# Attention and two mixture layers in one kernel: fills off GpSimd, a new order of first loads, a longer held-back tail

## The chip, the cores and the metric

The kernel runs on one core of one Trainium2 chip. The metric is the device time of one execution in microseconds (us); less is better.

## The reference

Three steps follow one another on 2304 tokens of width 512:

```python
attn_out = _attn_ref(q, k, v)            # 4 x 8 heads, 576 x 64, causal, window 64
x = moe(x): h = x @ w_in; r = relu(h); return (r * r) @ w_out       # 512 -> 2048 -> 512
x = moe2(x):
    do_compute = x @ w_skip > 0
    e_idx = argmax(x @ w_gate)           # 8 experts
    y[mask] = gate_w * (relu(x[mask] @ w1[e]) @ w2[e])              # 512 -> 1024 -> 512
    out[do_compute] = x + y
```

All of it is in float32; each float32 product is made of three matmuls on a high and a low half of the operands.

## The kernel before, in words

The tokens stand in 18 tiles of 128 (t), two tiles to a chunk (c, nine chunks). Engines are named as in the profile: PE (TensorE, with PEld for its weight loads), DVE (VectorE), ACT (ScalarE), POOL (GpSimd), SP (SyncE, which issues most loads).

**Opening (0 to about 45 us).** Attention of chunks 0 and 1 runs as eight groups (a tile and half of its heads). For one group: `at_qk` puts a mask (L261) and the scores (L278) into PSUM, DVE takes the maximum (L288, and the small L291 on 128x4), ACT the four exponentials (L302), DVE the sum and its reciprocal (L306, L308) and the product (L309). `at_tr` transposes the result on PE (L317) and copies it with ACT (L319). `at_pv` multiplies by v (L335), and ACT and DVE write the high and low half of the first layer's input `xt` (L343, L344).

In the same stretch the weights of the first mixture layer are converted from the 64-bit floats in which they come, in 32 halves (`conv_next`): ACT scales (L220), POOL clamps (L221), DVE does three integer steps on 128x512 (L223, L225, L227), ACT rounds to the high half (L233), POOL subtracts (L234). Behind each L234 a small POOL memset (L205) releases the load of a later half. `HOMES` says which of three buffers holds q and k of a tile; `load_next` loads the next tile into a buffer when it comes free. Tile 6 is the first that uses the zero-padded `qpad`, whose two 64x512 zero fills (L160, L161) are on POOL. `setup_routing` makes the constants of the routing step, and a 128x512 fill (L146) that a DMA from ACT's queue (L147) spreads over the routing table in DRAM.

**Middle.** For each chunk and each of eight units j: `l1` (first layer, 24 matmuls of 256 columns on L464 to L466, then relu L483, square L489, high half L490, low half L491) and, two units later, `l2` (12 matmuls of 512 columns, six for each tile). The results of `l1` stand in pool `gp`. Attention of later chunks and the routing are put between.

**Tail of the last chunk.** `l2` of the last `TAIL` units is held back. In a part whose order is written out by hand, tile 0 gets its six matmuls of each held-back unit first, then routing of tile 0 runs beside tile 1's matmuls. The first expert block follows.

**Experts (531 us to the end).** Each of eight experts has one block of 128 tokens (`static`), and extra blocks (`extras`) behind a branch, where more than 128 tokens go to it. A block begins with `ex_x`: four transposes (L818), a copy to the high half (L729) and a subtraction for the low half (L730), then the matmuls L831. In the profile three extra blocks run, one for expert 0 and two for expert 1.

The order of the instructions on each engine in the opening and the middle is set by a scheduler when the program is built; the engines then run their lists in that order.

Of the kernel before, what the change touches and what calls it, by code (L numbers as in the profile page):

```python
# [19 lines left out]
P = 128  # L20
# [27 lines left out]
DOT00 = 6  # L48
ROW = NE * NT
FILLS = ((2, 3), (1, 2), (1, 0), (2, 3), (2, 0), (0, 5))  # L50
TAIL = 3
FE = 1024
KF = FE // P
WIN = 64
# [8 lines left out]
def body(ctx, tc, qt_d, kt_d, vw_d, wi_d, wo_d, w9_d, w9r_d, w1_d, w2_d, out):  # L63
# [10 lines left out]
    small = pool("small", 4)  # L74
    xtp = pool("xtp", 2)
    rp = pool("rp", 2)
    gp = pool("gp", 3)
    dram = pool("dram", 1, space=DRAM)
    ps_h = pool("ps_h", 2, space=PSUM)
    ps_acc = pool("ps_acc", 1, space=PSUM)  # L80
# [15 lines left out]
    def sm():  # L96
        return sp.tile([P, 512], F32, tag="sm", name="sm")
# [35 lines left out]
            out=mask.rearrange("p a b -> p (a b)"), in_=maskb.rearrange("p a b -> p (a b)"))  # L133

    def setup_routing():
        nc.gpsimd.memset(ones, 1.0)
        nc.gpsimd.memset(tri, 1.0)
        nc.gpsimd.affine_select(
            out=tri, in_=tri, pattern=[[1, P]], compare_op=ALU.is_gt,
            fill=0.0, base=0, channel_multiplier=-1)  # L140
        nc.gpsimd.iota(io8i, pattern=[[1, NE]], base=0, channel_multiplier=0)
        nc.gpsimd.tensor_copy(out=io8, in_=io8i)
        nc.gpsimd.iota(route[:, :, 0], pattern=[[P, NT]], base=0, channel_multiplier=1)
        nc.gpsimd.memset(ohsum[:, 0, :], 0.0)
        fill = sm().bitcast(I32)
        nc.gpsimd.memset(fill, FAR)  # L146
        nc.scalar.dma_start(  # L147
            out=tab_v.rearrange("p r c -> p (r c)"), in_=fill[:, 0:2 * ROW])
        nc.scalar.dma_start(out=w9, in_=w9_d)
# [6 lines left out]
    def load_qk(t):  # L156
        i = home(t)
        k_ = kvs[i > 0].tile([P, NPAIR, P + WIN], F32, tag=f"k{i}", name="k")
        if t == len(HOMES):
            nc.gpsimd.memset(qpad[0:64, :, 1, :], 0.0)  # L160
            nc.gpsimd.memset(qpad[64:128, :, 0, :], 0.0)  # L161
        if t < len(HOMES):
            nc.sync.dma_start(
                out=q_s[i], in_=qt_d[t].rearrange("h d a b -> (h d) a b"))
        else:
            for h in range(2):
                nc.sync.dma_start(out=qpad[64 * h:64 * h + 64, :, h, :], in_=qt_d[t, h])
        nc.sync.dma_start(out=k_, in_=kt_d[t])
        kt_t[t] = k_

    def load_v(t):
        i = home(t)
        v_ = kvs[i > 0].tile([P, 2, DM], F32, tag=f"v{i}", name="v")
        nc.sync.dma_start(out=v_, in_=vw_d[t])
        vw_t[t] = v_

    def load_next(t, load):
        later = [n for n in range(t + 1, NT) if home(n) == home(t)]
        if later:
            load(later[0])  # L180
# [75 lines left out]
    def at_qk(t, g):  # L256
        s = bank("qk", t, g)
        i, k_ = home(t), kt_t[t]
        early = t // CT in EARLY
        if early:  # L260
            nc.tensor.matmul(  # L261
                s.rearrange("p (a b) -> p a b", a=2), lhsT=identb,
                rhs=mask_of(t, maskb).unsqueeze(1).to_broadcast([P, 2, 2 * P]),
                start=True, stop=False, skip_group_check=True)
        for pi in range(2):
            for blk in range(2):
                u = 2 * pi + blk
                pr = 2 * g + pi
                cols = slice(u * P, (u + 1) * P)
                if t >= len(HOMES):  # L270
                    nc.tensor.matmul(
                        s[:, cols], lhsT=qpad[:, 2 * pr + blk].rearrange("p a b -> p (a b)"),
                        rhs=k_[:, pr, 64 * blk:64 * blk + P],
                        start=not early, stop=True, skip_group_check=early)
                    continue
                for h in range(2):
                    half = slice(64 * h, 64 * h + 64)
                    nc.tensor.matmul(  # L278
                        s[half, cols], lhsT=q_s[i][half, 2 * pr + blk],
                        rhs=k_[half, pr, 64 * blk:64 * blk + P],  # L280
                        start=not early, stop=True, skip_group_check=early)
        if g == 1:
            load_next(t, load_qk)
        ef = sm()
        e = ef.rearrange("p (a b) -> p a b", a=4)
        nmx = small.tile([P, 4], F32, tag="nmx", name="nmx")
        if early:
            nc.vector.tensor_reduce(  # L288
                out=nmx, in_=s.rearrange("p (a b) -> p a b", a=4), axis=AX.X, op=ALU.max,
                negate=True)  # L290
            nc.vector.tensor_scalar(  # L291
                out=nmx, in0=nmx, scalar1=1.0 / 8.0, scalar2=None, op0=ALU.mult)
        else:
            mk = mask_of(t, mask)
            for u in range(4):
                nc.vector.tensor_tensor_reduce(  # L296
                    out=e[:, u, :], in0=s[:, u * P:(u + 1) * P],
                    in1=mk[:, u % 2 * P:(u % 2 + 1) * P], scale=-1.0 / 8.0, scalar=HUGE,
                    op0=ALU.add, op1=ALU.min, accum_out=nmx[:, u:u + 1])
        sums = small.tile([P, 4], F32, tag="sum", name="sum")  # L300
        for u in range(4):
            nc.scalar.activation(  # L302
                out=e[:, u, :], in_=s[:, u * P:(u + 1) * P] if early else e[:, u, :],
                func=AF.Exp, bias=nmx[:, u:u + 1],
                scale=1.0 / 8.0 if early else -1.0, accum_out=sums[:, u:u + 1])
        nc.vector.tensor_scalar(  # L306
            out=sums, in0=sums, scalar1=1e-9, scalar2=None, op0=ALU.add)
        nc.vector.reciprocal(out=sums, in_=sums)  # L308
        nc.vector.tensor_tensor(  # L309
            out=e, in0=e, in1=sums.unsqueeze(2).to_broadcast([P, 4, P]), op=ALU.mult)  # L310
        p_t[t, g] = e
# [287 lines left out]
    if True:  # L599
# [8 lines left out]
        load_qk(0)  # L608
        conv_load()
        load_qk(1)  # L610
        load_v(0)
        conv_load()
        load_qk(2)
        load_v(1)
        conv_load()
        load_v(2)
        conv_load()
        for _ in range(LOOK - 4):
            conv_load()
        setup_masks()  # L620
        acc_pool[1] = ps_s
        qk, tr, pv = grp_ops(0)
        qk1, tr1, pv1 = grp_ops(1)
# [3 lines left out]
        for s in range(10):  # L627
            if s < 8:
                qk[s]()
            if 1 <= s < 9:  # L630
                tr[s - 1]()
            if 2 <= s:
                pv[s - 2]()
            for _ in range(PRO[s]):
                conv_next()
            if s == 4:
                setup_routing()

        def w_free(kind, j):
            slot_q.extend((wp, w_tag[kind, j, h]) for h in range(2))  # L640
# [172 lines left out]

        def ex_x(tx, inner=True):
            xg = tx[2]
            pp = psa()
            for k in range(KD):
                nc.tensor.transpose(pp[:, k * P:(k + 1) * P], xg[:, k * P:(k + 1) * P], ident)  # L818
            return ex_split(pp, inner)

        def ex_block(e, tx, xt, fill=lambda i: None, nxt=lambda: None, late=False):
            ti, gw, xg, _ = tx
# [176 lines left out]
```

## Time and profile before

| | |
|---|---|
| time, median of 3 runs (lowest, highest) | 686.37 us (684.65, 687.01) |
| the profiled execution: its own time, its span | 685.27 us, 683.6 us |
| PE busy, share of the span | 656.6 us, 96% |
| DVE / ACT / POOL busy | 415.3 / 357.5 / 155.4 us |
| mean granted TensorE clock | 0.989 |
| DMA moved | 88.72 MB |

The span runs from the first to the last instruction. Idle time counts on the engine that the others wait for, here PE in most of the span; the mean hides that the first 45 us and the last 180 us look different from the middle.

### The profile page before, as it was taken

The page shows a single profiled execution, that of the slowest core. Times are in us where ns is not written, and L with a number is a line of the kernel's source. Part 1 is how long each engine was busy: PE and PEld are TensorE (multiplying, and loading weights), DVE is VectorE, ACT ScalarE, POOL GpSimd, SP SyncE. Part 2 cuts the span into 40 slices and gives each one's busy share as a digit, 9 for nine tenths or more (in the row PEclk, how much of TensorE's full clock was granted, in tenths as well). Part 3 has the DMA queues.
Part 4 walks back from the last instruction along what each step waited for, and adds up shares of the span by engine and source line. Part 5 has one row for each costly group of instructions (what it writes and reads, how often), then busy time and mean ns, then how long its engine had stood idle before and what let it go on. Part 6 is the DMA issues. An engine that isn't in the chain of part 4 may idle for free. (4 is left out here: it accounts for less than half of the span.)

```text
span 683.6 us, 12514 instructions
## 1 busy us (share of the span) xinstructions
PE 656.6 (96%) x4569; PEld 566.7 (83%) x4569; DVE 415.3 (61%) x1200; ACT 357.5 (52%) x821; POOL 155.4 (23%) x185
## 2 busy tenths in 40 slices
PE   7799999999999999999999999999999999999995
PEld 4588888989899889898989989899988777777774
DVE  4999977449627727716725824942735644288981
ACT  4887756544535444635535444544641544277761
POOL 5557666100100100000000000030001513044641
PEclk9899999999999999999999999999999999999998
DMA  8965453053203203203112121206592347559500
GB/s 332 349 206 172 147 168 111 1 203 98 70 32 102 70 32 101 70 32 102 40 61 85 48 71 50 83 26 230 177 317 100 111 151 279 224 161 337 222 12 8
DMA packets 45605, 88.72 MB, mean 130 GB/s; under 512 B 17806, under 2 KB 18062, under 8 KB 45392
## 3 DMA queue, kind: packets, MB, share of 16 engines
q1 hardware_dynamic: 42112, 83.38, 35.6%
q0 software_dynamic: 2976, 3.95, 1.8%
q8 instruction: 47, 0.77, 0.5%
q10 hardware_dynamic: 432, 0.32, 0.2%
q14 instruction: 38, 0.31, 0.1%
HBM read 79.07 MB, written 12.49 MB: 134 GB/s over the span
## 5 line engine op out<-in xcount | busy, mean ns | idle before, releaser
L464 PE MATMUL h<-xt,wi 128*128 128x256 f32 x576 | 165.3, 287 | 2.1 <-ACT r L480 2.1
L465 PE MATMUL h<-xt,wi 128*128 128x256 f32 x576 | 165.6, 287 | 0.3 <-DVE xt L344 0.3
L466 PE MATMUL h<-xt,wi 128*128 128x256 f32 x576 | 164.0, 285 | 0.0
L464 PE MATMUL acc<-wo,gh 128*128 128x512 f32 x288 | 116.3, 406 | 1.1 <-ACT gh L490 1.0
L464 PEld LDWEIGHTS h<-xt,wi 128*128 128x128 f32 x576 | 110.6, 192 | 6.4 <-ACT r L480 3.1
L465 PEld LDWEIGHTS h<-xt,wi 128*128 128x128 f32 x576 | 110.6, 192 | 3.4 <-DVE xt L344 0.6
L465 PE MATMUL acc<-wo,gh 128*128 128x512 f32 x288 | 112.6, 393 | 0.0
L466 PE MATMUL acc<-wo,gl 128*128 128x512 f32 x288 | 112.0, 393 | 0.0
L491 DVE TENSOR_TENSOR gl<-r,gh 128x512 fp32r<-128x512 f32 x72 | 52.4, 728 | 96.5 <-ACT gh L490 95.0
L466 PEld LDWEIGHTS h<-xt,wi 128*128 128x128 f32 x576 | 110.7, 192 | 0.0
L456 POOL DMA_INDIRECT tab_d<-route,posi x18 | 19.5, 1084 | 362.6 <-DVE posi L447 263.7
L483 ACT ACTIVATE r<-h 128x512 f32<-128x512 f32 x58 | 34.5, 595 | 98.4 <-PE h L466 94.7
L375 DVE CUSTOM_DVE_ANT_0 prod<-sm,w9b 128x512 f32<-128x512 f32 x108 | 74.0, 685 | 1.9 <-ACT sm L352 1.5
L466 PEld LDWEIGHTS acc<-wo,gl 128*128 128x128 f32 x288 | 54.1, 188 | 12.6 <-DVE gl L491 0.8
L464 PEld LDWEIGHTS acc<-wo,gh 128*128 128x128 f32 x288 | 54.1, 189 | 11.1 <-ACT gh L490 2.1
L465 PEld LDWEIGHTS acc<-wo,gh 128*128 128x128 f32 x288 | 54.3, 189 | 8.6 <-issue 0.2
L548 DVE TENSOR_TENSOR e_s<-e_s,e_s 128x1024 fp32r<-128x1024 f32 x34 | 42.1, 1258 | 11.9 <-ACT e_s L546 11.5
L302 ACT ACTIVATE sm<-sm,nmx 128x128 f32<-128x128 f32 x96 | 37.5, 392 | 20.7 <-DVE nmx L296 20.3
L319 ACT COPY sm<-a 128x512 f32<-128x512 f32 x36 | 21.4, 594 | 48.8 <-PE a L317 48.8
L489 ACT ACTIVATE r<-r 128x512 f32<-128x512 f32 x72 | 45.6, 634 | 1.5
L490 ACT CAST gh<-r 128x512 fp32r<-128x512 f32 x72 | 44.6, 619 | 1.5
L546 ACT CAST e_s<-e_s 128x1024 fp32r<-128x1024 f32 x42 | 42.9, 1050 | 2.5 <-PE acc L466 2.0
(205 smaller groups left out, 1144.6 us busy)
## 6 DMA issues: line engine op xcount, KB each, us to landing
e_s<-in_w_dram SPq DMA_DIRECT2D x54, 512.0 KB, 6.4
v<-in_vw_dram SPq DMA_DIRECT2D x18, 512.0 KB, 3.4
ri<-in_wi_dram SPq DMA_DIRECT2D x16, 512.0 KB, 4.1
ro<-in_wo_dram SPq DMA_DIRECT2D x16, 512.0 KB, 3.7
k<-in_kt_dram SPq DMA_DIRECT2D x18, 384.0 KB, 4.2
e_r<-in_w_dram SPq DMA_DIRECT2D x10, 512.0 KB, 6.6
x_d<-sm SPq DMA_DIRECT2D x17, 256.0 KB, 2.5
out_dram<-sm SPq DMA_DIRECT2D x17, 256.0 KB, 3.1
```

Of the source, the lines that this page charges most:

```text
L302: nc.scalar.activation(out=e[:, u, :], in_=s[:, u * P:(u + 1) * P] if early else e[:, u, :], func=AF.Exp, bias=nmx[:, u:u + 1], scale=1.0 ...
L319: nc.scalar.copy(out=pt, in_=pp)
L375: nc.vector.tensor_tensor_reduce(out=prod, in0=x2_t[t], in1=w9b_t[0][:, j, :], scale=1.0, scalar=0.0, op0=ALU.mult, op1=ALU.add, accum_out ...
L464: nc.tensor.matmul(out_ap, lhsT=ah, rhs=bh, start=start, stop=False)
L465: nc.tensor.matmul(out_ap, lhsT=ah, rhs=bl, start=False, stop=False)
L466: nc.tensor.matmul(out_ap, lhsT=al, rhs=bh, start=False, stop=stop)
L483: nc.scalar.activation(out=r, in_=hp.rearrange("p a b -> p (a b)"), func=AF.Relu)
L489: nc.scalar.activation(out=r, in_=r, func=AF.Square)
L490: nc.scalar.copy(out=ghf, in_=r)
L491: nc.vector.tensor_tensor(out=glf, in0=r, in1=ghf.bitcast(F32), op=ALU.subtract)
L546: nc.scalar.copy(out=hi, in_=raw)
L548: eng.tensor_tensor(out=lo, in0=raw, in1=hi.bitcast(F32), op=ALU.subtract)
```

## The change

Constants: `TAIL` goes from 3 to 4, pool `gp` from 3 to 4 buffers (the fourth holds the results of the one more unit), and the scratch of POOL's DMAs from 8192 to 4096 bytes.

```diff
     def setup_routing():
-        nc.gpsimd.memset(ones, 1.0)
-        nc.gpsimd.memset(tri, 1.0)
+        nc.vector.memset(ones, 1.0)
+        nc.vector.memset(tri, 1.0)
...
-        nc.gpsimd.memset(ohsum[:, 0, :], 0.0)
+        nc.vector.memset(ohsum[:, 0, :], 0.0)
         fill = sm().bitcast(I32)
-        nc.gpsimd.memset(fill, FAR)
+        nc.vector.memset(fill, FAR)
...
-        if g == 1:
+        if g == 1 and t != 2:
             load_next(t, load_qk)
+        if g == 1 and t == len(HOMES) - 1:
+            load_next(2, load_qk)
...
         load_qk(0)
         conv_load()
         load_qk(1)
+        conv_load()
         load_v(0)
+        load_qk(2)
         conv_load()
-        load_qk(2)
         load_v(1)
         conv_load()
         load_v(2)
-        conv_load()
         for _ in range(LOOK - 4):
             conv_load()
         setup_masks()
+        setup_routing()
...
-            if s == 4:
-                setup_routing()
...
         def ex_x(tx, inner=True):
             xg = tx[2]
+            if inner:
+                return ex_x_halves(xg)
...
+        def ex_x_halves(xg):
+            hi = gp.tile([P, 512], F32R, tag="gh", name="xh2")
+            lo = gp.tile([P, 512], F32R, tag="gl", name="xl2")
+            pps = [psa(), psa()]
+            cut = [slice(n * 256, (n + 1) * 256) for n in range(2)]
+            for n in range(2):
+                for k in range(2):
+                    nc.tensor.transpose(
+                        pps[n][:, k * P:(k + 1) * P],
+                        xg[:, (2 * n + k) * P:(2 * n + k + 1) * P], ident)
+                nc.scalar.copy(out=hi[:, cut[n]], in_=pps[n][:, 0:256])
+            for n in range(2):
+                nc.vector.tensor_tensor(
+                    out=lo[:, cut[n]], in0=pps[n][:, 0:256], in1=hi[:, cut[n]].bitcast(F32),
+                    op=ALU.subtract)
+            return hi, lo
```

`ex_x_halves` serves the extra blocks alone; a `static` block's tokens still go through `ex_x` whole. After the change the line numbers of the attention are two higher (L304 for L302, L321 for L319, L346 for L344 and so on).

The scheduler gives other lists for the opening. At three places:

**ACT, its first instructions.** `ri` is the raw half of a first-layer weight, `sm` the scores of a group. Before:

```order
L220 ACTIVATE ri_0_138<-ri_0_138 128x512
L302 ACTIVATE sm,sum<-s,nmx 128x128 x4
L220 ACTIVATE ri_1_145<-ri_1_145 128x512
L302 ACTIVATE sm,sum<-s,nmx 128x128 x4
L233 CAST wi_0_298<-f 128x512
L220 ACTIVATE ri_0_152<-ri_0_152 128x512
```

and now:

```order
L147 DMA tab_d<-sm 128x288
L220 ACTIVATE ri_0_138<-ri_0_138 128x512
L220 ACTIVATE ri_1_143<-ri_1_143 128x512
L304 ACTIVATE sm,sum<-s,nmx 128x128 x8
L233 CAST wi_0_309<-f 128x512
L220 ACTIVATE ri_0_150<-ri_0_150 128x512
L233 CAST wi_1_406<-f 128x512
L220 ACTIVATE ri_1_154<-ri_1_154 128x512
```

The scaling of the second weight half (L220 on `ri_1`) has moved ahead of the exponentials of the first two groups, the fourth ahead of the first copy L321, and the DMA of the routing table (L147) to the front.

**POOL, where `qpad` is zeroed.** Before:

```order
L221 TENSOR_SCALAR ri_1_156<-ri_1_156 128x512
L221 TENSOR_SCALAR ro_0_158<-ro_0_158 128x512
L161 MEMSET qpad 64x8x64
L160 MEMSET qpad 64x8x64
L234 TENSOR_TENSOR wi_0_507<-f,wi_0_507 128x512
L205 MEMSET ri_1_510 128x2
L146 MEMSET sm 128x512
L221 TENSOR_SCALAR ro_1_301<-ro_1_301 128x512
```

and now:

```order
L221 TENSOR_SCALAR ro_0_158<-ro_0_158 128x512
L221 TENSOR_SCALAR ro_1_312<-ro_1_312 128x512
L234 TENSOR_TENSOR wi_1_576<-f,wi_1_576 128x512
L205 MEMSET ro_0_579 128x2
L161 MEMSET qpad 64x8x64
L160 MEMSET qpad 64x8x64
L221 TENSOR_SCALAR ri_0_409<-ri_0_409 128x512
L221 TENSOR_SCALAR ri_1_504<-ri_1_504 128x512
```

The fill `sm` (L146) is gone from here. The two fills of `qpad` stand behind the subtraction of the fourth weight half, and before it stand two clamps.

**DVE, from the third to the fourth half of `xt`.** Before:

```order
L344 TENSOR_TENSOR xt<-xp,xt 128x2x128
L291 TENSOR_SCALAR nmx<-nmx 128x4
L227 SCALAR_TENSOR_TENSOR f<-ro_0_158,h_118 128x512
L308 RECIPROCAL sum<-sum 128x4
L288 TENSOR_REDUCE nmx<-s 128x4
L344 TENSOR_TENSOR xt<-xp,xt 128x2x128
```

and now:

```order
L346 TENSOR_TENSOR xt<-xp,xt 128x2x128
L310 RECIPROCAL sum<-sum 128x4
L223 TENSOR_SCALAR h_118<-ri_0_409 128x512
L290 TENSOR_REDUCE nmx<-s 128x4
L311 TENSOR_TENSOR sm<-sm,sum 128x512
L225 SCALAR_TENSOR_TENSOR h_118<-ri_0_409,h_118 128x512
L293 TENSOR_SCALAR nmx<-nmx 128x4
L227 SCALAR_TENSOR_TENSOR f<-ri_0_409,h_118 128x512
L346 TENSOR_TENSOR xt<-xp,xt 128x2x128
```

Between the same two rows there now stand a whole conversion (three wide steps on `ri_0`) and a product L311. Over the opening DVE's list has, ahead of the product of the eighth group (L309, now L311), 29 conversion steps where it had 21, eight maxima and eight products as before, and five writes of `xt` where it had six. On PE, 24 first-layer matmuls of 256 columns stand ahead of the eighth group's transposes where 36 stood.

## Rows read from the trace of the kernel before

**Rows 1.** Busy time by stretch: us, busy (instructions) of each engine, TensorE clock, DMA share, GB/s.

```profile
0.00:45.00 45.00, 35.38 (x344) 25.68 (x345) 34.25 (x74) 30.64 (x103) 23.47 (x51) 0.89 0.86 304
45.00:500.00 455.00, 453.37 (x3354) 406.99 (x3354) 277.02 (x982) 236.83 (x596) 72.92 (x96) 1.00 0.29 94
500.00:531.00 31.00, 29.87 (x225) 25.84 (x224) 12.88 (x54) 8.18 (x16) 4.85 (x5) 1.00 0.57 205
```

**Rows 2.** Timeline of TensorE: start, us, engine, line, [idle before it and its releaser].

```profile
28.89 0.38 PE L261 MATMUL s<-maskb,identb 128*128 128x512 bf16 x1 [1.47 <-ACT sm L302]
...
42.02 0.28 PE L465 MATMUL h<-xt,wi 128*128 128x256 f32 x1
42.14 0.28 PE L466 MATMUL h<-xt,wi 128*128 128x256 f32 x1
...
42.97 0.66 PE L317 MATMUL a<-ident,sm 128*128 128x128 f32 x4
```

**Rows 3.** Two stretches of 2 us, columns as in the first group.

```profile
10.00:12.00 2.00, 1.40 (x17) 0.94 (x17) 2.00 (x7) 1.06 (x5) 0.00 (x0) 1.00 1.04 413
...
32.00:34.00 2.00, 1.73 (x9) 1.46 (x10) 2.00 (x7) 1.94 (x10) 0.45 (x1) 0.50 1.11 342
```

**Rows 4.** Timeline of VectorE in the opening.

```profile
7.88 0.69 DVE L288 TENSOR_REDUCE nmx<-s 128x4 f32<-128x512 f32 x1 [6.63 <-PE s L278]
...
14.78 0.54 DVE L291 TENSOR_SCALAR nmx<-nmx 128x4 f32<-128x4 f32 x1
...
24.34 2.90 DVE L291 TENSOR_SCALAR nmx<-nmx 128x4 f32<-128x4 f32 x1
...
27.87 0.69 DVE L225 SCALAR_TENSOR_TENSOR h<-ri,h 128x512 int32<-128x512 int32 x1
28.47 0.16 DVE L306 TENSOR_SCALAR sum<-sum 128x4 f32<-128x4 f32 x1
...
35.17 0.84 DVE L291 TENSOR_SCALAR nmx<-nmx 128x4 f32<-128x4 f32 x1
...
41.91 0.69 DVE L309 TENSOR_TENSOR sm<-sm,sum 128x512 f32<-128x512 f32 x1
```

**Rows 5.** Timeline of GpSimd beside VectorE's long wait.

```profile
24.32 0.52 POOL L160 MEMSET qpad<- 64x512 f32 x1
24.81 1.27 POOL L234 TENSOR_TENSOR wi<-f,wi 128x512 fp32r<-128x512 f32 x1
...
26.06 0.52 POOL L146 MEMSET sm<- 128x512 int32 x1
26.56 0.66 POOL L221 TENSOR_SCALAR ro<-ro 128x512 f32<-128x512 f32 x1
```

**Rows 6.** Timeline of ScalarE in the opening.

```profile
8.87 0.37 ACT L302 ACTIVATE sm<-s,nmx 128x128 f32<-128x128 f32 x1 [1.01 <-DVE nmx L291]
...
11.32 0.69 ACT L220 ACTIVATE ri<-ri 128x512 f32<-128x512 f32 x1 [0.94 <-DMA ri<-in_wi_dram]
```

**Rows 7.** Timeline of TensorE at the end of the last chunk.

```profile
512.28 0.39 PE L466 MATMUL acc<-wo,gl 128*128 128x512 f32 x1
513.68 0.50 PE L464 MATMUL acc<-wo,gh 128*128 128x512 f32 x1 [1.00 <-ACT gh L490]
```

**Rows 8.** Timeline of ScalarE there.

```profile
511.40 1.05 ACT L546 CAST e_xt<-e_s 128x1024 fp32r<-128x1024 f32 x1
...
513.01 0.62 ACT L490 CAST gh<-r 128x512 fp32r<-128x512 f32 x1
```

**Rows 9.** Timeline of TensorE at the start of an extra block.

```profile
570.10 0.63 PE L818 MATMUL a<-ident,sm 128*128 128x128 f32 x4 [0.95 <-DVEq L900]
571.45 0.50 PE L831 MATMUL h<-e_xt,xh 128*128 128x512 f32 x1 [0.72 <-ACT xh L729]
```

**Rows 10.** Timeline of ScalarE: the copy of 512 columns there.

```profile
570.81 0.59 ACT L729 CAST xh<-a 128x512 fp32r<-128x512 f32 x1 [2.65 <-PE a L818]
```

**Rows 11.** Timeline of ScalarE: a copy of 256 columns in the opening.

```profile
28.72 0.38 ACT L343 CAST xt<-xp 128x256 fp32r<-128x256 f32 x1
```

More of the change, by code (lines that the diff above doesn't have):

```diff
@@ L50 @@
 FILLS = ((2, 3), (1, 2), (1, 0), (2, 3), (2, 0), (0, 5))
-TAIL = 3
+TAIL = 4
 FE = 1024
@@ L76, in body @@
     rp = pool("rp", 2)
-    gp = pool("gp", 3)
+    gp = pool("gp", 4)
     dram = pool("dram", 1, space=DRAM)
@@ L983 @@
     nc = bacc.Bacc("TRN2", target_bir_lowering=False, num_devices=1,
-                   dynamic_dma_scratch_size=8192)
+                   dynamic_dma_scratch_size=4096)
     arrays, args = {}, []
```

## The prediction

> **What bounds the kernel now.** I read the busy time by stretch first, because the mean over the span hides where there is anything to win. From 45 to 500 us TensorE is busy for 453.37 of 455.00 us at full clock, so 1.6 us are idle there; from 500 to 531 us it is 29.87 of 31.00 [rows 1]. No edit can win in the middle. In the first 45 us TensorE is busy for 35.38, idle for 9.6, and its mean granted clock is 0.89 [rows 1]. That stretch, the end of the last chunk and the starts of the expert blocks are the three places that the change touches, and I take them one by one.
>
> In the opening, look at two stretches: from 10 to 12 us the DMA queues are full (413 GB/s), and from 32 to 34 us TensorE is granted 0.50, its 1.2 GHz level [rows 3], after a stretch with holes: the largest ended at 28.89, 1.47 us long, behind the exponentials [rows 2]. Then ask who paces it. The opening ends for TensorE with the eighth group's transposes at 42.97, which stand behind VectorE's eighth product, 41.91 to 42.60 [rows 2, 4]. So I follow VectorE from its first maximum at 7.88 to 42.5: 34.6 us. A wide step takes 0.60 at its pace (27.87 to 28.47) [rows 4]; its list holds 37 wide steps there (21 conversion steps, eight maxima, eight products), 22.2 us, and about 4.2 us of `xt` writes and small steps. It works for 26.4 us and stands for 8.2.
>
> Part of that standing is one small instruction, L291 on 128x4. A step of that size takes 0.16 (L306), but L291 took 2.90, 0.84 and 0.54 at three places [rows 4], 3.8 us over the normal price. During the longest GpSimd ran without a gap, and L291 ended at 27.24, when GpSimd's last clamp of that run did (26.56 + 0.66) [rows 4, 5].
>
> **Scale.** The profiled execution took 685.27 us and the median is 686.37, 1.1 higher. The sum is made against 685.27, and 1.1 is added at its end. A measurement of this kernel can tell some 0.3% from no change, 2.06 us: below 684.3 is faster, above 688.4 slower.
>
> **End of the last chunk.** TensorE waits 1.00 us there for the high half `gh` of the last unit [rows 7]. ScalarE writes it from 513.01 to 513.63, behind a cast of 1.05 us for the next expert's weights [rows 8]. With four units held back instead of three, tile 0's matmuls of one more unit stand ahead of that wait: six of about 0.24 us (512 columns, at twice the 0.12 from 42.02 to 42.14 for 256 [rows 2]), 1.4 us of work which is not new, only moved. So the wait is covered, and about 0.1 that follows it for the low half: -1.1, with bounds from -1.1 to 0 (nothing, if the cast still stands ahead of `gh`). The fourth `gp` buffer costs no time. Two loads of expert weights move behind stores on SyncE's queue, but are used some 80 us later: 0. The early gather of tile 0 has up to 0.5 us less slack; what covers it is the matmul work of tile 1, and if that ran out the cost would be that 0.5.
>
> **Extra blocks.** From the first transpose of a block to its first matmul now pass 1.35 us: 570.10 to 571.45, of which 0.72 is idle behind the copy [rows 9]. The copy of 512 columns takes 0.59 [rows 10], one of 256 columns 0.38 [rows 11]. With halves the first copy starts when two of the four transposes are done, and the first matmul needs that half alone: about -0.18 for two transposes and -0.21 for the copy, 0.4 a block. Three extra blocks run. For expert 0's a full copy for the next block goes ahead on ScalarE, so I count 0.2 there: 0.4 + 0.4 + 0.2, -1.0, bounds -1.2 to 0. One more copy and one more subtraction a block lie beside the matmuls: 0.
>
> **Opening, what is added.** VectorE's list now has 29 conversion steps ahead of the eighth product where it had 21, and one `xt` write fewer: 8 x 0.60 - 0.3 = +4.5. TensorE has 24 first-layer matmuls ahead of the eighth transposes where it had 36; what no longer fills holes runs later, 12 x 0.12 (42.02 to 42.14) [rows 2]: +1.4. The fills now on VectorE stand ahead of 7.88, where it waited 6.63 us for scores [rows 4]: 0. On ScalarE the second weight half's scaling now stands ahead of the first exponentials, which began at 8.87; it began at 11.32, when its data landed [rows 6]. The `v` load moves behind it, 512 KB at 413 GB/s or 1.27 us earlier, and the table's fill of 144 KB moves in front, 0.36 later; so about 10.4, and the exponentials of the first groups come about 11.0. Eight exponentials of 0.37 then follow without a break, to 14.0; before, the second four came behind the scaling, from 12.01 to 13.5. So they end 0.5 later, and VectorE has conversion steps to fill that time. I count it among the stalls below. TensorE may start later by up to the 2 us, which the same holes hold.
>
> **Opening, what is taken.** Three instructions of 0.52 like L160 and L146 leave GpSimd's run beside L291 [rows 5]: the two `qpad` fills move behind the fourth subtraction, the routing fill to VectorE. By the row L291 waited for the whole run, so it gets 3 x 0.52 shorter: -1.6. The other 6.6 us in which VectorE stood (8.2 less 1.6) have nothing to do in the list of before; in the new one eight conversion steps stand among them. All of them filled would be -6.6, none 0. No row tells which, and I take half, -3.3.
>
> The opening: 4.5 + 1.4 - 1.6 - 3.3 = +1.0. Its bounds: if nothing is filled and the fills were not what L291 waited for, +5.9; if VectorE never stands, -2.3.
>
> What L291 waits for can be read in a second way. The row shows 2.90 us across the ends of four GpSimd instructions, at about 24.8, 26.1, 26.6 and 27.2 [rows 5]. The Trainium skill, "SBUF — State Buffer", section "SBUF: two separate sides", says that VectorE and GpSimd lock their shared pair of ports for one whole instruction and the other blocks; by it L291 would get in at the first end, after 0.5 us. By that rule the removed fills would be worth nothing and the sum would be 1.6 higher. The trace doesn't agree with a lock that is let go at each end, and I go by the row.
>
> The scratch of GpSimd's DMAs at half the size: the trace of before shows no stall that it could lengthen, and only a few of these DMAs are under way at once; 0, and up to 0.5 for the gathers of an expert if it turns them into a wait.
>
> **Sum.** 685.27 + 1.0 - 1.1 - 1.0 = 684.2 in the profiled execution's scale, 685.3 in that of the median.
>
> **Rivals.**
>
> *Fills were not the cause.* L291 waited for the clamps and subtractions in that run, and these are still there: 685.3 + 1.6 = 686.9, still within 0.3%. Chance 0.06, counted with the forecast below.
>
> *Faster: the opening gets shorter.* All three long L291 go, so the other 2.2 us of their price are won whole instead of half (-1.1), and with fewer holes TensorE is not granted 0.50 from 32 to 34 us [rows 3], which costs 1.0 there at half speed: 685.3 - 2.1 = 683.2, between 681.5 and 684.3 as more of VectorE's standing is filled. For it: the routing's GpSimd work goes to the start, where GpSimd is idle. Against: in the new lists more VectorE work precedes each group, and groups pace TensorE. Chance 0.36.
>
> *Slower: a new long wait of the small step.* GpSimd now runs two clamps, the subtraction of the fourth half and both `qpad` fills one behind another: 2 x 0.66 + 1.27 + 2 x 0.52 = 3.6 us [rows 5], where it ran for 2.9 beside the L291 of before. If the L291 (now L293) of the fifth or sixth group falls to its start, it waits for all of it, VectorE's longer list stands behind it, and exponentials, transposes and `xt` follow. Then nothing of 1.6 is won, and of the 6.6 only 1.1 instead of 3.3: opening +4.8, 685.3 + 3.8 = 689.1, between 688.4 and 690.5. It decides when VectorE still stands for more than 6.4 of its 8.2 us in all before the eighth product: then the opening is 5.9 - 1.8 = 4.1 longer, and the sum 688.4. For it: the fills are still on GpSimd, and the clamps come together now. Against: the place moved away from a maximum by some steps. Chance 0.26.
>
> *The change doesn't do what it says.* The `qpad` fills stay on GpSimd, so "off GpSimd" holds for the routing fills alone; and if other blocks than the three ran, the term of 1.0 would change. Both are inside the cases above.
>
> **The numbers.** Forecast 685.3 us with 0.38 for within 0.3% (684.3 to 688.4), which contains the case of 686.9; faster 0.36; slower 0.26. The faster case reaches down to 681.5 and the slower up to 690.5; leaving out 0.1 at either end gives 682.3 to 689.3. The likeliest case alone spans 684.3 to 687.5.
>
> **What would show it.** Right: the product of the eighth group ends at 43 to 45 us, the transposes stand about 1 to 2 us later than 42.97, TensorE idle in the first 47 us is about 10 to 11; the longest L293 is 1.4 us or less; TensorE's wait for `gh` in the last chunk is under 0.2; a matmul of an extra block follows the first transpose after 0.95. Wrong, faster: eighth transposes before 42 us and no stretch at 0.50. Wrong, slower: an L293 of 3 us or longer, and eighth transposes after 46.5. Wrong elsewhere: TensorE busy for less than 452 of 455 us in the middle, because a buffer of `gp` or a load came late; or a new idle stretch at the first expert's gather.

## The result, and the profile after

| | before | after |
|---|---|---|
| time, median of 12 runs each (lowest, highest) | 685.49 us (682.5, 687.51) | 689.65 us (687.6, 691.14) |
| the profiled execution: its own time, its span | 685.27, 683.6 | 689.03, 687.3 |

Ratio after to before 1.0064, 95% interval 1.0047 to 1.0081: slower by 4.2 us. The forecast was 685.3 and the range ended at 689.3, so the time lies 0.35 above it.

Busy time by stretch of the profile after, which answers to [rows 1], and two stretches of 6 us:

```profile
0.00:45.00 45.00, 29.85 (x284) 20.26 (x285) 35.16 (x78) 29.23 (x99) 26.06 (x52) 0.85 0.87 305
45.00:500.00 455.00, 452.16 (x3361) 405.82 (x3361) 267.71 (x954) 231.78 (x590) 66.94 (x89) 1.00 0.28 91
500.00:531.00 31.00, 31.00 (x205) 27.46 (x204) 15.35 (x58) 12.52 (x22) 3.50 (x4) 1.00 0.58 202
...
36.00:42.00 6.00, 2.22 (x26) 1.74 (x26) 5.97 (x14) 5.12 (x16) 2.88 (x6) 0.98 0.88 322
42.00:48.00 6.00, 5.53 (x42) 4.86 (x44) 5.92 (x13) 4.84 (x18) 4.46 (x6) 0.50 0.65 235
```

In the first 45 us TensorE is busy for 29.85 where it was 35.38, and its clock is lower, 0.85; between 500 and 531 us no idle time is left. Of the 455 us between, 2.8 are idle (1.6 before), so nearly the whole loss lies ahead of the middle. The last transposes of attention, far behind the opening, show how much; of before and of after:

```profile
453.42 0.60 PE L317 MATMUL a<-ident,sm 128*128 128x128 f32 x4
```

```profile
461.73 0.60 PE L319 MATMUL a<-ident,sm 128*128 128x128 f32 x4
```

The change is 8.3 us behind here, and 3.7 at the end of the span; 4.6 come back in the tail, the experts and the end of the span. To see where the 8.3 come from, read ScalarE, VectorE and TensorE of after in the order of the chain. ScalarE first (lines 220 are the scaling of the first and of the second weight half, L304 the first group's first exponential):

```profile
7.61 0.67 ACT L220 ACTIVATE ri<-ri 128x512 f32<-128x512 f32 x1 [4.88 <-DMA ri<-in_wi_dram]
10.88 0.65 ACT L220 ACTIVATE ri<-ri 128x512 f32<-128x512 f32 x1 [2.60 <-DMA ri<-in_wi_dram]
11.44 0.35 ACT L304 ACTIVATE sm<-s,nmx 128x128 f32<-128x128 f32 x1
...
36.38 0.71 ACT L220 ACTIVATE ro<-ro 128x512 f32<-128x512 f32 x1 [1.75 <-DMA ro<-in_wo_dram]
...
37.70 0.39 ACT L304 ACTIVATE sm<-s,nmx 128x128 f32<-128x128 f32 x1
```

The scaling of the second half now stands ahead of the first exponentials. It waits 2.60 us for its transfer, and everything behind it on ScalarE waits too: the first exponential starts at 11.44, before at 8.87 [rows 6], though VectorE has written the maxima that it needs by 8.33 (L293, 8.16 + 0.17). VectorE then, of after, and its first product of before:

```profile
12.96 0.17 DVE L308 TENSOR_SCALAR sum<-sum 128x4 f32<-128x4 f32 x1 [2.15 <-ACT sm L304]
...
15.07 1.66 DVE L311 TENSOR_TENSOR sm<-sm,sum 128x512 f32<-128x512 f32 x1
...
20.38 0.90 DVE L293 TENSOR_SCALAR nmx<-nmx 128x4 f32<-128x4 f32 x1
...
45.41 0.68 DVE L311 TENSOR_TENSOR sm<-sm,sum 128x512 f32<-128x512 f32 x1
```

```profile
11.88 0.68 DVE L309 TENSOR_TENSOR sm<-sm,sum 128x512 f32<-128x512 f32 x1
```

VectorE stands for 2.15 us for these exponentials, and its first product comes at 15.07 (before at 11.88, 3.2 us earlier), its eighth at 45.41 (before at 41.91 [rows 4], 3.5 earlier). L293 (L291 before) takes 0.90 at most. TensorE last, of after, and its first two holes of before:

```profile
12.98 0.58 PE L261 MATMUL s<-maskb,identb 128*128 128x512 bf16 x1 [4.24 <-ACT sm L304]
...
42.47 1.09 PE L319 MATMUL a<-ident,sm 128*128 128x128 f32 x4 [3.27 <-DVE sm L311]
...
44.57 0.58 PE L466 MATMUL h<-xt,wi 128*128 128x256 f32 x1
...
48.49 0.69 PE L319 MATMUL a<-ident,sm 128*128 128x128 f32 x4
```

```profile
10.43 0.38 PE L261 MATMUL s<-maskb,identb 128*128 128x512 bf16 x1 [1.26 <-ACT sm L302]
...
13.45 0.46 PE L261 MATMUL s<-maskb,identb 128*128 128x512 bf16 x1 [1.62 <-ACT sm L302]
```

A hole of 4.24 us opens behind the late exponentials, where before two of 1.26 and 1.62 stood, and one of 3.27 ahead of the seventh group's transposes. Ahead of that second hole VectorE is busy for 5.97 of the 6 us from 36 to 42, and six conversion steps stand between its sixth and its seventh product: TensorE waits there for VectorE's list, not for data. Behind it the clock falls to 0.50 from 42 to 48 us, and the eighth group's transposes start at 48.49, 5.5 later than before [rows 2]. In the first 55 us TensorE is idle for 15.2 us (9.6 before). That is 5.5 of the 8.3; the lower clock accounts for about the rest (2.7, an estimate from busy time and granted clock of each stretch of 6 us).

### The profile page after: what moved, and what is told of

Read it like the earlier page. It is cut to its first block, busy times and chain, and to the rows that moved or that the text cites. A ratio compares the mean times of both kernels' runs of the same rounds, so it can differ in the third digit from the quotient of the medians.

```text
span 687.3 us, 12519 instructions
## 1 busy us (share of the span) xinstructions
PE 658.3 (96%) x4569; PEld 567.4 (83%) x4569; DVE 414.3 (60%) x1207; ACT 356.7 (52%) x824; POOL 149.2 (22%) x181
## 5 line engine op out<-in xcount | busy, mean ns | idle before, releaser
L550 DVE TENSOR_TENSOR e_s<-e_s,e_s 128x1024 fp32r<-128x1024 f32 x35 | 47.4, 1374 | 13.8 <-ACT e_s L548 13.3
L304 ACT ACTIVATE sm<-sm,nmx 128x128 f32<-128x128 f32 x96 | 37.5, 392 | 20.7 <-DVE nmx L298 20.3
L321 ACT COPY sm<-a 128x512 f32<-128x512 f32 x36 | 21.1, 585 | 46.1 <-PE a L319 46.1
```

Source lines behind the costliest of these rows:

```text
L304: nc.scalar.activation(out=e[:, u, :], in_=s[:, u * P:(u + 1) * P] if early else e[:, u, :], func=AF.Exp, bias=nmx[:, u:u + 1], scale=1.0 ...
L321: nc.scalar.copy(out=pt, in_=pp)
L550: eng.tensor_tensor(out=lo, in0=raw, in1=hi.bitcast(F32), op=ALU.subtract)
```

## The experiments

Fourteen kernels, each timed in turn with before on the same chip. "First exp." is the start of the first exponential, "conv." the number of conversion steps ahead of VectorE's eighth product, "idle" TensorE's idle time in the first 55 us, "last transposes" the milestone above; these are from one profile each, or from the lists. The medians of before that stand beside e1 to e14 lie between 684.7 and 685.4.

| kernel | median, us | ratio to before (95%) | first exp. | conv. | 8th product | idle | last transposes |
|---|---|---|---|---|---|---|---|
| before | 685.5 | | 8.87 | 21 | 41.91 | 9.6 | 453.42 |
| after | 689.7 | 1.0064 (1.0047, 1.0081) | 11.44 | 29 | 45.41 | 15.2 | 461.73 |
| e1 tail and halves | 681.0 | 0.994 (0.992, 0.996) | 8.68 | 21 | 40.41 | 10.1 | 452.90 |
| e2 loads alone | 696.1 | 1.0174 (1.0148, 1.0199) | 10.69 | 27 | 44.93 | 16.5 | 463.11 |
| e3 all but the loads | 677.9 | 0.9901 (0.9877, 0.9925) | 8.59 | 20 | 38.49 | 8.9 | 450.38 |
| e4 after, scaling back | 683.2 | 0.998 (0.9965, 0.9995) | 8.81 | 24 | 41.86 | 12.5 | 457.46 |
| e5 after, VectorE's order back | 692.1 | 1.0113 (1.0084, 1.0141) | 11.37 | 21 | 46.95 | 17.1 | 464.84 |
| e6 after, both back | 676.6 | 0.9871 (0.9841, 0.9902) | 8.44 | 21 | 38.65 | 9.7 | 449.84 |
| e7 tail and scratch | 681.6 | 0.9955 (0.9933, 0.9977) | 8.87 | 21 | 40.06 | 13.1 | 452.76 |
| e8 opening without loads | 681.9 | 0.9957 (0.9944, 0.9969) | 8.43 | 20 | 38.26 | 10.2 | 450.19 |
| e9 e3, scaling first | 694.5 | 1.0127 (1.0108, 1.0146) | 12.24 | 30 | 51.12 | 18.8 | 467.79 |
| e10 two scalings back | 677.7 | 0.9877 (0.9851, 0.9903) | 8.46 | 20 | 39.54 | 10.0 | 452.22 |
| e11 fills alone | 682.6 | 0.9955 (0.9939, 0.9972) | 8.72 | 20 | 38.60 | 9.0 | 450.47 |
| e12 e6, load not deferred | 684.1 | 0.9984 (0.9969, 0.9999) | 8.85 | 21 | 38.77 | 13.7 | 457.29 |
| e13 scratch alone | 683.6 | 0.998 (0.9965, 0.9995) | 8.79 | 21 | 40.53 | 11.2 | 453.07 |
| e14 halves alone | 682.5 | 0.9955 (0.9939, 0.9971) | 8.90 | 21 | 42.07 | 12.6 | 454.74 |

Before, e1, e7, e13 and e14 have the same lists in the opening, and still their profiles lie between 40.06 and 42.07 at the eighth product and between 9.6 and 13.1 in idle time; e7, with the most, had a clock of 1.00 in these 55 us, before 0.91. So two profiles that differ by no more than that show nothing, and idle time and clock have to be read together; the medians decide. A difference between two kernels of the table can be one of medians from different chips; if each is taken against its own runs of before, it changes by up to 0.8 us.

### Which part of the change costs it

**e1, tail and halves** is before with these lines of the change, the opening's list unchanged:

```diff
-TAIL = 3
+TAIL = 4
-    gp = pool("gp", 3)
+    gp = pool("gp", 4)
-                   dynamic_dma_scratch_size=8192)
+                   dynamic_dma_scratch_size=4096)
+            if inner:
+                return ex_x_halves(xg)
```

> The opening of before word for word, with the fourth held-back unit (and its buffer, and the small scratch) and the halves of the extra blocks. Both theories: TensorE's 1.00 us wait for gh at the end of the last chunk is gone and each extra block starts 0.2 to 0.5 us earlier, as in the profile of the change; 2.0 us less than before, about 683.5 us, ratio 0.997. If the small scratch or the moved weight loads cost something, it shows here as 685.5 or more.

Measured 681.03 us, 3.7 below before. These parts are a gain, and a larger one than their terms.

**e2, loads alone**, is before with

```diff
         load_qk(1)
+        conv_load()
         load_v(0)
+        load_qk(2)
         conv_load()
-        load_qk(2)
         load_v(1)
         conv_load()
         load_v(2)
-        conv_load()
```

> Before, with the new order of the first loads alone. Theory A (the order of the loads makes the scheduler write another list for every engine, and this list is what costs 8.3 us in the opening): the opening is 7 to 9 us longer, TensorE idle about 15 us in the first 54 us instead of 9.5, time 6 to 9 us above before, ratio 1.009 to 1.013. Theory B (the fills and the routing moved to the front, or the deferred load of tile 2's buffer, cost it): within 1 us of before.

Measured 696.06, 11.4 above before; TensorE is idle for 16.5 us in the first 55. **e3** is the change with these lines put back:

> The change with the old order of the first loads; all else as changed (fills on VectorE, routing at the front, deferred load, four held-back units, halves). Theory A: VectorE's list has 20 conversion steps ahead of the eighth product, as before 21, so the opening is within 1 us of before and the time 2 to 3 us below before, ratio 0.995 to 0.997. Theory B: 3 to 5 us above before, as the change.

Measured 677.88, 6.8 below before and 11.8 below the change. So the order of the first loads, with the lists that come with it, costs 11.4 to 11.8 us, and all else is a gain; theory B falls. Both sizes were underestimated.

### What about the loads costs it

The new order lets the scheduler write other lists. Two differences in them were candidates: on ScalarE the scaling ahead of the exponentials, on VectorE 29 conversion steps ahead of the eighth product where 21 stood. Edges that hold one instruction behind another on the same engine put each back without touching the loads. **e4** (x_i is the last exponential of a group, n counts the weight halves):

```diff
+        exp_i.append(x_i)
...
-        nc.scalar.activation(out=hf, in_=hf, func=AF.Copy, scale=F64_SCALE)
+        with tc.issue_after(exp_i[0].ins) if n == 1 else ExitStack():
+            nc.scalar.activation(out=hf, in_=hf, func=AF.Copy, scale=F64_SCALE)
```

> The change with one edge more: the scaling of the second weight half is issued on ScalarE behind the first group's exponentials, as before. Loads stay in the new order. Theory A1 (ScalarE's queue, in which the exponentials wait for a weight that lands at 10.9 us, makes the hole of 4.2 us on TensorE and all that follows): at least 4 of the 8.3 us come back, time 685.5 or less, ratio to before 1.000 or below. Theory A2 (VectorE's eight conversion steps more ahead of the eighth product cost it): only the hole's 1 to 1.5 us come back, ratio 1.003 to 1.006.

Measured 683.23, 6.4 below the change. The one edge changed VectorE's list too: 24 conversion steps stand ahead of its eighth product, 29 in after. ScalarE's rows in its profile (L309 exponentials of the first and the second group, L225 the scaling):

```profile
8.81 0.37 ACT L309 ACTIVATE sm<-s,nmx 128x128 f32<-128x128 f32 x1
...
10.99 0.68 ACT L225 ACTIVATE ri<-ri 128x512 f32<-128x512 f32 x1 [0.67 <-DMA ri<-in_wi_dram]
11.56 0.36 ACT L309 ACTIVATE sm<-s,nmx 128x128 f32<-128x128 f32 x1
```

The transfer lands as in after, but the first exponentials no longer wait for it. **e5** puts VectorE's order back instead (prod_i holds the products):

```diff
+        late = {3: 3, 4: 4, 5: 5, 6: 6, 7: 7}
+        with tc.issue_after(prod_i[late[n]].ins) if n in late else ExitStack():
             nc.vector.tensor_scalar(
                 out=fp, in0=hw, scalar1=3, scalar2=None, op0=ALU.logical_shift_left)
...
```

> The change with five edges more on VectorE: the conversions of the fourth to eighth weight half are issued behind the products of groups 4 to 8, so that 21 conversion steps stand ahead of the eighth product as before, not 29. ScalarE's scaling stays ahead of the first exponentials. Theory A2 (the steps ahead of the products cost it): 5 us or more of the 11.8 between the change and the version with the old load order come back, ratio to before 0.999 or below. Theory A1 (the late start behind ScalarE's queue costs it, and it is carried on): 0 to 2 us come back, ratio 1.004 to 1.007.

Measured 692.14, which is 2.5 above the change, not below: a miss of both theories, and A2 falls as the whole cause. Its rows on ScalarE say why; L224 is a scaling, L310 the first exponential of the eighth group:

```profile
44.44 0.67 ACT L224 ACTIVATE ri<-ri 128x512 f32<-128x512 f32 x1 [3.12 <-DMA ri<-in_wi_dram]
45.01 0.35 ACT L310 ACTIVATE sm<-s,nmx 128x128 f32<-128x128 f32 x1
```

A conversion that comes later releases the load of a later half later (the memset L205 stands behind it), and that half's scaling still stands ahead of the exponentials: ScalarE waits 3.12 us for the transfer, and the eighth group with it: its small step on VectorE (L299) ends at 43.35, its exponentials start at 45.01. It is the same trap at another place. After has such a wait too, 1.75 us at 36.38, but there it can hold the exponentials behind it for 0.5 us at most (L293 ends at 37.22, they start at 37.70). **e6** has both edges:

> The edges of both: scaling behind the first group's exponentials, and the conversions behind the products. Lists nearly those of the version with the old load order, loads in the new order. Theory A (the lists cost it, not the order of the transfers): within 2 us of that version, 677.9, so ratio to before 0.990 to 0.993. Rival (the later v and q, k loads cost it by themselves): stays at 682 or more, ratio 0.996 to 1.000.

Measured 676.61, 13.0 below the change and 1.3 below e3: with lists like those of before the new order of the loads costs nothing. The gain is larger than expected (0.990 to 0.993). Row of its first 55 us, where TensorE is idle for 9.65 and the clock is 0.97:

```profile
0.00:55.00 55.00, 45.35 (x439) 33.45 (x440) 47.13 (x97) 40.38 (x128) 31.54 (x61) 0.97 0.85 296
```

The change, e4, e5 and e6 are the four ways to set two places, the scaling on ScalarE and the five conversions on VectorE:

| | VectorE without the five edges | with the five edges |
|---|---|---|
| scaling ahead of the exponentials | 689.7 (after) | 692.1 (e5) |
| scaling behind them | 683.2 (e4) | 676.6 (e6) |

So VectorE's order makes about half of the 13.0 us between the change and e6. While the scaling stands first, putting the conversions back gains nothing; with the scaling back it gives 6.6 us. And with the conversions back the place on ScalarE is worth 15.5 us instead of 6.4, though part of the 15.5 is the second trap that e5 has. The fourth product shows how VectorE's order costs: 12 conversion steps stand ahead of it in e4, nine in e6. Of e4 (VectorE, TensorE), then of e6:

```profile
25.09 1.05 DVE L317 TENSOR_TENSOR sm<-sm,sum 128x512 f32<-128x512 f32 x1
```

```profile
26.20 0.66 PE L326 MATMUL a<-ident,sm 128*128 128x128 f32 x4 [2.09 <-DVE sm L317]
```

```profile
21.96 0.68 DVE L319 TENSOR_TENSOR sm<-sm,sum 128x512 f32<-128x512 f32 x1
```

In e4 TensorE stands for 2.09 us for this product; in e6 it does not stand for it.

**e9** is the converse: e3, so the old loads, with one edge that holds the first group's exponentials behind the second half's scaling.

```diff
+        hf1 = raw_q[1][0][:, :, 1].bitcast(F32)
+        pre_i.append(nc.scalar.activation(out=hf1, in_=hf1, func=AF.Copy, scale=F64_SCALE))
...
-        for u in range(4):
-            nc.scalar.activation(
+        with tc.issue_after(pre_i[0].ins) if t + g == 0 else ExitStack():
+            for u in range(4):
+                nc.scalar.activation(
```

> The version with the old load order (677.9 us), with one edge that puts the scaling of the second weight half ahead of the first group's exponentials on ScalarE; the loads stay in the old order, so that this half lands later still. Theory A1 (the one place in ScalarE's queue makes the list and the loss; the order of the transfers by itself does nothing): VectorE's list again has some 30 conversion steps ahead of the eighth product, the first product comes at 15 us or later, and the time is 8 to 13 us above that version, 686 to 691, ratio to before 1.002 to 1.009. Rival (the new order of transfers is needed for the loss): at most 3 us above it, 681 or less, ratio 0.995 or below.

Measured 694.54, 16.7 above e3 where 8 to 13 were expected, and the rival falls. 30 conversion steps stand ahead of the eighth product, so the one place on ScalarE is enough to bring the rest of the list; the 16.7 are the price of both. The first product comes at 14.18, not at 15 or later. Its rows on ScalarE (L629 the scaling, L308 the first exponential), on TensorE, and two stretches:

```profile
11.69 0.65 ACT L629 ACTIVATE ri<-ri 128x512 f32<-128x512 f32 x1 [3.88 <-DMA ri<-in_wi_dram]
12.24 0.35 ACT L308 ACTIVATE sm<-s,nmx 128x128 f32<-128x128 f32 x1
```

```profile
13.78 0.59 PE L264 MATMUL s<-maskb,identb 128*128 128x512 bf16 x1 [5.05 <-ACT sm L308]
```

```profile
42.00:48.00 6.00, 3.68 (x22) 2.79 (x24) 5.93 (x11) 4.48 (x18) 2.96 (x4) 0.50 0.64 232
48.00:54.00 6.00, 4.49 (x39) 3.96 (x36) 5.84 (x12) 4.92 (x12) 3.99 (x6) 0.50 0.66 218
```

With the old order the half lands later, ScalarE waits 3.88 us, the hole on TensorE is 5.05, and the clock is 0.50 for twelve us later on. In the table every kernel whose first exponential starts later than 10 us takes 689 us or more, and every other one 685.5 or less.

**e10** tries to go further: the scaling of the second half behind the second group's exponentials, that of the third behind the third's.

```diff
-        with tc.issue_after(exp_i[0].ins) if n == 1 else ExitStack():
+        sc = {1: 1, 2: 2}
+        with tc.issue_after(exp_i[sc[n]].ins) if n in sc else ExitStack():
```

> Try for a faster version: as both orders (676.6 us), but the scaling of the second half behind the second group's exponentials and that of the third behind the third's. If waiting for landed weights ahead of exponentials is what costs, the 0.75 and 1.65 us that ScalarE still waits there go: 674 to 676, ratio 0.984 to 0.988. If the weights are then late for the first layer's matmuls: 678 or more.

Measured 677.65, no better than e6 (676.61; the intervals overlap). **e12** is e6 with the load of tile 2's buffer not deferred:

```diff
-        if g == 1 and t != 2:
+        if g == 1:
             load_next(t, load_qk)
-        if g == 1 and t == len(HOMES) - 1:
-            load_next(2, load_qk)
```

> As both orders (676.6 us), with the load of tile 2's buffer not deferred. If the deferral gives nothing here: within 1 us of 676.6, ratio 0.986 to 0.989; if it matters with the new load order, because a weight load then stands behind a buffer that is not free: 678 or more.

Measured 684.09, 7.5 above e6. The reason isn't the one that was expected: SyncE's queue looks the same, and the eighth product is on time. The loss lies later, in rows of ScalarE (L309 an exponential of the ninth group, L352 the high half of `xt`) and TensorE:

```profile
46.55 0.37 ACT L309 ACTIVATE sm<-a,nmx 128x128 f32<-128x128 f32 x1 [1.44 <-DVE nmx L298]
...
47.60 0.38 ACT L352 CAST xt<-xp 128x256 fp32r<-128x256 f32 x1
```

```profile
48.03 0.39 PE L473 MATMUL h<-xt,wi 128*128 128x256 f32 x1 [2.39 <-ACT xt L352]
```

Here the ninth group's exponentials, which wait 1.44 us for VectorE, stand ahead of the cast that TensorE's next first-layer matmul needs: a wait of 2.39. Whether the deferral itself or only the list that comes with it makes this, no run separates. With the old loads it made no difference (e8 against e11, below).

### What the gains are made of

**e7** is before with the tail, its buffer and the scratch; **e8** before with the fills on VectorE, the routing at the front and the deferred load; **e11** is e8 without the deferral:

```diff
-        nc.gpsimd.memset(ones, 1.0)
-        nc.gpsimd.memset(tri, 1.0)
+        nc.vector.memset(ones, 1.0)
+        nc.vector.memset(tri, 1.0)
...
         setup_masks()
+        setup_routing()
...
-            if s == 4:
-                setup_routing()
```

> Before, with the fourth held-back unit alone (buffer and scratch with it). By the profiles 1.1 us of waiting for gh go; then what the experts' weight loads give: 1 to 2.5 us below before, ratio 0.9965 to 0.9985. If the halves make most of the 3.7 us of both, this one stays within 0.5 us of before.

> Before, with the fills on VectorE, the routing at the front and the deferred load, no other edit. Theory: the fill of 0.52 and the routing's other GpSimd steps leave the stretch in which the small step L291 waited 2.9 us; 2 to 3.5 us below before, ratio 0.995 to 0.997. If what L291 waits for is the clamps and subtractions (the fills were worth nothing): within 1 us of before.

> Before, with the fills on VectorE and the routing at the front; the load of tile 2's buffer not deferred. If the fills made the 2.9 us of the run with both: 681 to 682.5, ratio 0.994 to 0.997. If the deferral made them: within 1 us of before.

e8 measured 681.86 and e11 682.61, 2.9 and 2.4 below their runs of before, so the deferral adds nothing that can be told here. In e11's profile the small step beside GpSimd's run is 1.69 (2.90 before [rows 4]), and VectorE's eighth product comes at 38.60, 3.3 earlier (1.5 to 3.5 earlier than in the five profiles with the lists of before):

```profile
24.57 1.69 DVE L291 TENSOR_SCALAR nmx<-nmx 128x4 f32<-128x4 f32 x1
```

e7 measured 681.61, 3.2 below, more than expected (1 to 2.5). Its trace, like all others with 4096 bytes of scratch, ends sooner behind GpSimd's last DMA issue. **e13** is before with the scratch alone, **e14** with the halves alone:

> Before, with the scratch of GpSimd's DMAs at 4096 bytes and nothing else. Theory: the stretch behind GpSimd's last DMA issue, 4.9 us in every trace with 8192 and 3.3 in every one with 4096, hangs on the scratch; that stretch becomes 3.3, the lists stay as before, and the time is 1.5 us below before, ratio 0.9965 to 0.999. Rival (the fourth held-back unit or the gp buffer makes it): the stretch stays at 4.9 us and the time within 0.5 us of before.

> Before, with the halves of the extra blocks alone. By the starts of the three blocks in the profile of the change (0.22, 0.43 and 0.48 us less idle): 0.9 to 1.2 us below before, ratio 0.998 to 0.9995. If the second copy and subtraction delay something in the block: the same as before or above.

e13 measured 683.59, 1.8 below before. The last issue of GpSimd in before (span 683.6) and in e13 (span 681.2):

```profile
677.73 0.97 POOL L880 DMA_INDIRECT out_dram<-xg,tabs  x1 [10.05 <-DVE xg L878]
```

```profile
676.88 0.98 POOL L880 DMA_INDIRECT out_dram<-xg,tabs  x1 [10.05 <-DVE xg L878]
```

From the end of that row to the end of the span pass 4.9 us in before and 3.3 in e13: the scratch makes it, not the tail. It leaves 1.4 of e7's 3.2 for the tail, by medians whose intervals reach 1.0 and 1.5 us to either side. e14 measured 682.49, 2.9 below, nearly three times what was expected of it. The starts of the blocks show only 1.1; the rest is in weight waits of later experts. Of before, and of e14:

```profile
628.92 0.86 PE L831 MATMUL h<-e_s,xh 128*128 128x512 f32 x3 [1.01 <-issue]
...
642.63 0.60 PE L841 MATMUL a<-ident,r 128*128 128x128 f32 x4 [1.53 <-ACT e_s L546]
```

```profile
640.56 0.27 PE L860 MATMUL a<-ident,r 128*128 128x128 f32 x1 [0.25 <-issue]
```

2.5 us of such waits in before, one of 0.25 in e14. They differ from kernel to kernel (e1 has 0.56 and 1.34, e7 1.28 and 1.04), so how much of this belongs to the halves stays open.

## Why the prediction was wrong

**The step that failed** is the one on ScalarE in the opening: "the exponentials of the first groups come about 11.0 ... they end 0.5 later, and VectorE has conversion steps to fill that time. I count it among the stalls below. TensorE may start later by up to the 2 us, which the same holes hold." The time was about right (11.44), its price of nothing was not. The prediction weighed the end of the eighth exponential; the first product hangs on the fourth, which ends at 12.83 instead of 10.28. And VectorE had no steps to fill the time: from its first maximum to its first product it is busy for 4.44 of 7.63 us, in before for 3.52 of 4.00. The start of a chain was taken for one of its stalls: exponentials, product, transposes and the next group's scores follow one another, so the 3.2 us by which the first product was late stood as 3.5 us at the eighth. e4 gives 6.4 us back by an edge at this one place, and between e5 and e6, whose edits differ in it alone, lie 15.5.

**VectorE's steps.** 4.5 of added work less 1.6 and 3.3: from the first to the eighth product pass 30.03 us in before and 30.34 in after, though 25 conversion steps stand between them, before 18. Beside before the sum had the size about right, and its upper bound, in which nothing is filled, was not reached: VectorE's standing shrank, as these rows of before and of after show (busy time is in the order TensorE, its weight loads, VectorE, ScalarE, GpSimd).

```profile
11.88:42.60 30.72, 24.18 (x253) 19.50 (x254) 28.00 (x60) 24.02 (x87) 14.87 (x22) 0.83 0.90 315
```

```profile
15.07:46.09 31.02, 22.35 (x232) 16.58 (x229) 30.70 (x65) 24.21 (x80) 19.27 (x28) 0.83 0.84 293
```

But the steps were not free. They took what the fills had given: with the same fills e3, with 17 steps between the two products, needs 26.95 us, and e6, with 18, needs 27.20. e4, with 21, needs 30.03 and is 6.6 us slower than e6. Against e3 the eighth product of the change is 6.9 later, 3.5 by its start and 3.4 by the way. That price is the second part that the sum did not have. e5 cannot show it, because there the group behind the late scaling waits.

**TensorE's fewer matmuls**, +1.4: the way from the eighth product to the transposes grew from 1.06 to 3.08 us, with 0.50 granted from 42 to 48. The sum counted the work that is left over, not that it would run at the lower clock. It is a third part that was missing; the faster rival had only the opposite.

**The fills**, -1.6: right in sign, and the rows bear the mechanism out as far as they go. The waits of L291 beyond its normal 0.16, of those that took more than 0.3, sum to 3.8 us in before and 1.2 in after; e11 is 2.4 below before. The reading of the Trainium skill, "SBUF — State Buffer", section "SBUF: two separate sides", by which the fills were worth nothing, was the worse one here; the waits shrank and the time fell. e11 moves the other routing steps too, so it isn't a test of the fills alone.

**Tail**, -1.1: the wait for `gh` is gone, and e7 less e13 gives -1.4. **Scratch**, 0 to +0.5: wrong in sign, it measured -1.8, and the row behind the last DMA issue that it changes was not looked at. **Extra blocks**, -1.0: the starts came 1.1 earlier in e14 (0.22, 0.43 and 0.43 less idle), as the sum had it; the whole was -2.9, and the rest of that is open. In after the idle ahead of the second such block's first matmul fell from 0.72 [rows 9] to 0.29:

```profile
577.20 0.63 PE L831 MATMUL a<-ident,sm 128*128 128x128 f32 x4 [0.95 <-DVEq L920]
578.12 0.50 PE L851 MATMUL h<-e_xt,xh 128*128 128x512 f32 x1 [0.29 <-ACT xh L834]
```

**The rivals.** The slower one gave 689.1 with a chance of 0.26, near the 689.65, but not by its mechanism: the longest L293 is 0.90, where it asked for 3 us or more. It was a price of the right size for another cause. Its condition on VectorE, more than 6.4 us of standing, was met: counted as the prediction counts, 38.6 us from the first maximum to the end of the eighth product less 30.9 of work leave 7.7. But the sum saw one pool of standing that added steps could fill, and a large part of it lay at the head, ahead of the first product. The faster case was right in sign for all but the loads: e3 gives 677.9, below the whole range. Of the signs the eighth product ended at 46.1 (43 to 45 were named), and the transposes came 5.5 later (1 to 2).

## What to carry to other kernels

In these traces ScalarE ran its list in order: the first exponentials, whose maxima were there at 8.33, stood until 11.44 behind a scaling whose data came late. So an instruction that is fed by a transfer and moved one place ahead of the head of a chain makes the whole chain wait for that transfer: compare the landing time with the start of what stands behind it, at each such place. A delay at the head of a chain that paces a stretch is to be carried to the stretch's end in full; stalls absorb added work, not a late start. Work that they absorb is not free either: it takes the room that another edit has freed, here the fills. And two places in two lists can depend on each other, so that putting one back alone shows nothing or a loss (e5): try both together. Where a scheduler writes the lists, an edit of the order of loads is an edit of every engine's list; an edge that puts one instruction back tells the two apart, and here the change with two such edges (e6) is the fastest version measured, 676.6 us, 1.3% below before.

## What was not expected of the hardware

The size of the scratch for GpSimd's DMAs sets a part of the end: from GpSimd's last DMA issue to the end of the span pass 4.9 us in each trace with 8192 bytes (before, e2, e8, e11, and e14) and 3.3 in each with 4096. Why it does stays open.

The granted clock of the opening moves between executions of the same list: before has 0.56 from 30 to 36 us; e1, with the same opening, has 1.00 there and 0.54 from 12 to 18, and e7 has 1.00 in both. The last transposes lie up to 2 us apart (452.76 in e7, 454.74 in e14) with the same lists in the opening, so single profiles of the opening are compared to no less than that.
